# Joined half groups, one ReLU and one subtract moved off VectorE, and a new order at both ends of a top-k attention and highway kernel

## The chip, the cores and the metric

The kernel runs on one core of one Trainium2 chip. The metric is the device time of one execution in microseconds (us), as a median of several runs. Lower is better. TensorE, VectorE (DVE in the profile), ScalarE (ACT), GpSimd (POOL) and SyncE (SP) each take their own instructions in order, and an instruction waits where a semaphore tells it to.

## The reference

The inputs are q, k and v of shape (8 batches, 8 heads, 576 rows, 64), and the weights of one highway layer. Per batch and head the kernel computes the scores, keeps in every row those that reach the row's 32nd largest, and takes the softmax over them:

```python
scores = scale * np.matmul(q, k.transpose(0, 1, 3, 2))
kth = np.partition(scores, -32, axis=-1)[..., -32:-31]
scores = np.where(scores >= kth, scores, -1e9)
attn = softmax(scores) @ v
```

The heads are put side by side, giving x of shape (4608, 512), and the layer follows:

```python
H = np.maximum(x @ w_h, 0.0)
T = 1.0 / (1.0 + np.exp(-(x @ w_t + b_t)))
out = T * H + (1.0 - T) * x
```

## The kernel before, in words

**Tiling.** The 576 query rows of a batch are cut into four groups of 128 rows (`qt` 0 to 3) and a *rest group* of 64 rows (`qt` 4). A full group has 8 tiles, one per head; a rest group has 4 tiles, each holding two heads of 64 rows. Two tiles make a *pair*, two pairs a *quad*. A batch has 18 pairs, so 144 pairs in all, and a written-out loop walks over `step` n = 0 to 149. Pair n passes through stages in successive steps: `scores` and `evac` (step n-1), `tree` (n), `lists` and `lists_rest`, `mask` and `trans` (n+4), `av` (n+5).

**Selecting the 32nd largest.** VectorE does this. `tree` and `folds` take maxima of halves, giving tiles `hi`, `hh`, `h3` (printed as h) and `w2` (printed as w). `minima`, on GpSimd, gets the matching minima with four integer operations per quad at each odd step: hh, hh, hi, hi. `tops` (even steps) and `rest` (odd steps, the last rounds in the next even step as `late`) pull the 8 largest of each list by MAX8 and MATCH_REPLACE8. `settle` keeps, on GpSimd, figures that let the end of the kernel decide whether the lists were long enough; if not, an exact version of the whole kernel runs after it.

**The layer.** When a group's last pair has passed `av`, `norm` divides by the row sums (reciprocal `rinv` on VectorE, the product `x` on GpSimd). Then three pieces are put into the list `ffn`, and each step pops one: `ffn_x` (transposes of x on TensorE; xT and xh on ScalarE), `ffn_h` with `ffn_d` (first product on TensorE, then d = relu(product) - xh by one VectorE instruction), `ffn_t` with `ffn_e` and `ffn_o` (second product, tanh on ScalarE, d = (tanh+1)*d on VectorE, o = x + d on GpSimd, and the store on SP). The TensorE half of a piece (`pre`) stands early in a step, the rest (`post`) late.

**What sets the order.** All compute instructions are pinned to program order on their engine (class `Pinned`). DMAs and the instructions issued before the loop are not. So on GpSimd an instruction written in `post` of an odd step stands behind the four `minima` of that step. I number steps from the first pair of a batch: with n mod 18, full groups reach `norm` at 8, 12, 16 and 20, and the rest group at 22 (which is 4 in the next batch). Its pieces are popped at 24, 25 and 26 (6, 7 and 8 in the next batch), because the group ahead of it uses 21 to 23. So the rest group's `ffn_d` comes at an odd step and its `ffn_e` at the even step right after, while a full group's `ffn_d` comes at an even step.

**Both ends.** At the start, the four head pairs of batch 0 are prepared one after another (`early`): loads of k, q and v (twelve DMAs for each head pair), transposes of k and q through one PSUM buffer (`fps`, one buffer, shared with the layer), copies on ScalarE, and then the scores of the next pair. At the end, after the last pair, the layer of the last full group and of the last rest group runs alone, followed by the checks.

Of the kernel before, what the change touches and what calls it, by code (L numbers as in the profile page):

```python
# [18 lines left out]
WIDE = 600.0  # L19
# [27 lines left out]
class Group:  # L47


    def __init__(self, b, qt, gi, H, P):  # L50
        self.b, self.qt, self.gi = b, qt, gi
        self.rem = qt == J
        self.qlen = P // 2 if self.rem else P
        tiles = (
            [(2 * hp, 2 * hp + 1) for hp in range(H // 2)]
            if self.rem
            else [(h,) for h in range(H)]
        )
        self.nt = len(tiles)
        self.pairs = [tiles[i : i + 2] for i in range(0, self.nt, 2)]  # L60


class Ops:
# [31 lines left out]
    def load_pair(self, src, hp, name, eng=None):  # L95
        nc, D, S, R, P = self.nc, self.D, self.S, self.R, self.P
        JP = J * P
        t = self.ldpool.tile([P, J + 1, 2, D], FP32, tag=name, name=name)
        eng = eng or nc.sync
        for hh in range(2):  # L100
            h = 2 * hp + hh
            eng.dma_start(
                t[:, 0:J, hh, :], src(h, 0, JP).rearrange("(p j) d -> p j d", j=J)
            )
            eng.dma_start(t[0:R, J, hh, :], src(h, JP, S))
        return t
# [6 lines left out]
    def prep_pair(self, srcs, hp, prep, qeng=None):  # L113
# [6 lines left out]
        def load():  # L120
            ins["k"] = self.load_pair(srcs[1], hp, "kin")
            ins["q"] = self.load_pair(srcs[0], hp, "qin", qeng)
            ins["v"] = self.load_pair(srcs[2], hp, "vin")

        def main(name, dst):
            kqps = self.fps.tile([P, 512], FP32, tag="fp", name="kqps")
            for c in range(J):
                nc.tensor.transpose(
                    kqps[:, c * P : (c + 1) * P],
                    ins[name][:, c, :, :].rearrange("p h d -> p (h d)"),  # L130
                    self.ident[:],
                )
            nc.scalar.copy(dst[:, hp, 0:JP], kqps[:])

# [11 lines left out]
        def values():  # L146
            vdst = vb[:, 2 * hp : 2 * hp + 2, :, 0:D].rearrange("p h c d -> p c h d")
            nc.scalar.copy(vdst[:, 0:J], ins["v"][:, 0:J])
            nc.scalar.copy(vdst[0:R, J], ins["v"][0:R, J])
# [51 lines left out]
    def folds(self, k, g, pi):  # L201


        vec, P, S, H = self.nc.vector, self.P, self.S, self.H
        H1, H2, H3 = S // 2, S // 4, S // 8
        if pi == 0:
            g.w2 = self.lpool.tile([P, H, H2 + 24], FP32, tag="w2", name="w2")
        hi, hh, h3 = self.quads[k]
        vec.tensor_tensor(hh[:], hi[:, :, 0:H2], hi[:, :, H2:H1], ALU.max)
        a, b = hh[:, :, 0:H3], hh[:, :, H3:H2]  # L210
        vec.tensor_tensor(h3[:], a, b, ALU.max)
        return vec.tensor_tensor(
            g.w2[:, 2 * pi : 2 * pi + 4, H3:H2], a, b, ALU.min
        )
# [22 lines left out]
    def tops(self, g, t, h3, hl):  # L237
# [5 lines left out]
        m1, m2, w2 = g.m1[:, t, :], g.m2[:, t, :], g.w2[:, t, :]  # L243
# [13 lines left out]
    def rest(self, g, t, lo):  # L257
# [6 lines left out]
        w2 = g.w2[:, t, :]  # L264
# [29 lines left out]
    def lists(self, n, g, pi):  # L294
        P, H = self.P, self.H
        if pi == 0:
            for name in ("m1", "m4") if self.exact else ("m1", "m2", "m4"):
                setattr(g, name, self.lpool.tile([P, H, 8], FP32, tag=name, name=name))
# [19 lines left out]
    def settle(self, g):  # L318
# [7 lines left out]
            self.room[:, g.gi, 0:nt, 0:3],  # L326
            thr.unsqueeze(2).to_broadcast([P, nt, 3]),
# [3 lines left out]
        gp.tensor_tensor(  # L331
            self.slack[:, g.gi, 0:nt, 0], g.m2[:, 0:nt, 7], thr, ALU.subtract
        )
        gp.tensor_copy(self.reach[:, g.gi, 0:nt], g.m1[:, 0:nt, 0])
# [44 lines left out]
    def trans(self, n):  # L379
# [4 lines left out]
        zr = self.zrps.tile([P, 512], FP32, tag="zr", name="zr")  # L384
        for ti in range(2):
            self.chunk_T(zr[:, ti * P : (ti + 1) * P], z, pen, ti, J)
        nc.scalar.activation(
            et[:, :, J, :],
            zr[:, 0 : 2 * P].rearrange("p (t j) -> p t j", t=2),
            AF.Exp,  # L390
            scale=self.scale,
        )
# [10 lines left out]
        self.st[n].update(et=et, zr=zr)  # L403

    def av(self, n, g, pi, vb):
# [4 lines left out]
        if pi == 0:  # L410
            g.xs = self.xpool.tile([P, self.H * DE], FP32, tag="xs", name="xs")
        ql = g.qlen
        c0 = col = 0 if g.rem else 2 * P
        h0 = g.pairs[pi][0][0]
        for ti, heads in enumerate(g.pairs[pi]):
            for hi, h in enumerate(heads):
                q0 = hi * (P // 2)
                for c in range(J + 1):
                    nc.tensor.matmul(
                        zr[0:ql, col : col + DE],  # L420
# [6 lines left out]
        nc.scalar.copy(g.xs[0:ql, h0 * DE : h0 * DE + col - c0], zr[0:ql, c0:col])  # L427
# [3 lines left out]
    def norm(self, g):  # L431
        nc, P, H, D = self.nc, self.P, self.H, self.D
        ql = g.qlen
        xs3 = g.xs[0:ql, :].rearrange("p (h e) -> p h e", e=D + 1)
        rinv = self.xpool.tile([P, H], FP32, tag="rinv", name="rinv")
        nc.vector.reciprocal(rinv[0:ql, :], xs3[:, :, D])
        g.x = self.xpool.tile([P, H * D], FP32, tag="x", name="x")
        nc.gpsimd.tensor_tensor(
# [6 lines left out]
    def ffn_x(self, g):  # L445
        nc, P, n_g, ql = self.nc, self.P, self.n_g, g.qlen
# [16 lines left out]
    def ffn_h(self, g):  # L463
        nc, P, n_g, ql = self.nc, self.P, self.n_g, g.qlen
# [10 lines left out]
    def ffn_d(self, g):  # L475

        ql = g.qlen
        g.d = self.fpool.tile([self.P, self.dm], FP32, tag="d", name="d")
        self.nc.vector.scalar_tensor_tensor(
# [8 lines left out]
    def ffn_t(self, g):  # L488

        nc, P, n_g, ql = self.nc, self.P, self.n_g, g.qlen  # L490
        g.ps = self.fps.tile([P, 512], FP32, tag="fp", name="tps")
# [13 lines left out]
    def ffn_e(self, g):  # L505

        ql = g.qlen
# [9 lines left out]
    def ffn_o(self, g, dst):  # L517
        ql = g.qlen
        o = self.fpool.tile([self.P, self.dm], FP32, tag="o", name="o")
        self.nc.gpsimd.tensor_tensor(o[0:ql, :], g.x[0:ql, :], g.d[0:ql, :], ALU.add)  # L520
        self.nc.sync.dma_start(dst, o[0:ql, :])
# [3 lines left out]
def kernel(  # L525
# [17 lines left out]
    assert D == 64 and R == 64 and H % 4 == 0 and dm == 512  # L543
# [13 lines left out]
    nc.vector.tensor_scalar_mul(nident[:], ident[:], -STEEP)  # L557
# [11 lines left out]
    for i in range(2):  # L569
# [5 lines left out]
    room = const([P, NG, H, 3], FP32, "room")  # L575
    nc.gpsimd.memset(room[:], 1.0)
    slack = const([P, NG, H, 1], FP32, "slack")
    nc.gpsimd.memset(slack[:], 1.0)
    reach = const([P, NG, H], FP32, "reach")
    nc.gpsimd.memset(reach[:], 1.0)  # L580
# [8 lines left out]
        room=room, slack=slack, reach=reach,  # L589
    )  # L590

    with ExitStack() as cm:
# [12 lines left out]
        def srcs(b):  # L605
            return [
                (lambda h, r0, r1, t=t: t[b, h, r0:r1, :]) for t in (q, k, v)
            ]

        def out_rows(g):  # L610
            if not g.rem:
                r0 = g.b * S + g.qt
                return out[r0 : r0 + JP : J, :]
            r0 = g.b * S + JP
            return out[r0 : r0 + R, :]

        groups = [
            Group(b, qt, b * nck + qt, H, P) for b in range(B) for qt in range(nck)
        ]
        pairs = [(g, pi) for g in groups for pi in range(len(g.pairs))]  # L620
# [6 lines left out]
        def prep(b, hp, qeng=None):  # L627
            if hp == 0:
                preps[b] = ops.prep_alloc(vbufs[b % 2])
            return ops.prep_pair(srcs(b), hp, preps[b], qeng)  # L630
# [20 lines left out]
        early = [prep(0, hp, nc.scalar if hp == 0 else None) for hp in range(NHP)]  # L651
# [8 lines left out]
        step = 0  # L660
        late = []
        while step < NPR + 6 or ffn:
            n = step
            if n + 1 < NHP:
                for piece in early[n + 1][1:4]:
                    piece()
                if n + 2 < NHP:
                    early[n + 2][0]()
            if have(n):
                ops.tree(n)  # L670
                if n % 2:
                    ops.minima(n // 2, ops.folds(n // 2, *pairs[n - 1]))
            if n == 1:
# [3 lines left out]
            post = None  # L677
            if ffn:
                pre, post = ffn.pop(0)
                pre()  # L680
# [3 lines left out]
            if have(n - 4):  # L684
# [7 lines left out]
            ended = have(n - 5) and pairs[n - 5][1] == len(pairs[n - 5][0].pairs) - 1  # L692
# [8 lines left out]
            else:  # L701
# [3 lines left out]
                if post:  # L705
                    post()
                if ended:
                    ops.norm(pairs[n - 5][0])
                ops.run(gens)
            if have(n - 4):  # L710
# [7 lines left out]
            if ended:  # L718
# [6 lines left out]
                        lambda g=g: (ops.ffn_e(g), ops.ffn_o(g, out_rows(g))),  # L725
# [3 lines left out]


        ok = const([P, 4], FP32, "ok")
        vec = nc.vector
        vec.tensor_reduce(ok[:, 0:1], room[:], op=ALU.min, axis=AX.XYZ)
        vec.tensor_reduce(ok[:, 1:2], slack[:], op=ALU.min, axis=AX.XYZ)
        vec.tensor_reduce(ok[:, 2:3], reach[:], op=ALU.max, axis=AX.XY)
        bad = const([P, 4], FP32, "bad")
        vec.tensor_scalar(bad[:, 0:1], ok[:, 0:1], TINY, None, ALU.is_lt)
        vec.tensor_scalar(bad[:, 1:2], ok[:, 1:2], 0.0, None, ALU.is_lt)
        vec.tensor_scalar(bad[:, 2:3], ok[:, 2:3], WIDE, None, ALU.is_gt)
        vec.tensor_reduce(bad[:, 3:4], bad[:, 0:3], op=ALU.max, axis=AX.X)  # L740
        bps = ops.fps.tile([P, 512], FP32, tag="fp", name="bps")
        nc.tensor.transpose(bps[0:1, 0:P], bad[:, 3:4], ident[:])
        flag_f = const([1, 1], FP32, "flag_f")
        vec.tensor_reduce(flag_f[:], bps[0:1, 0:P], op=ALU.max, axis=AX.X)
        flag = const([1, 1], I32, "flag")
        vec.tensor_copy(flag[:], flag_f[:])

    taken = nc.values_load(flag[0:1, 0:1], min_val=0, max_val=1)
    with tc.If(taken > 0):
        with tc.For_i(0, B, 1) as b:  # L750
            with ExitStack() as cm:
                ops = Ops(cm, tc, shared, exact=True)
                srcs = [
                    (lambda h, r0, r1, t=t: t[bass.ds(b, 1), h, r0:r1, :].rearrange("o s d -> (o s) d"))
# [58 lines left out]
```

## Time and profile before

| | us |
|---|---|
| median of 3 runs | 925.96 |
| lowest, highest | 923.73, 926.5 |
| the profiled run, timed | 925.72 |
| span of its trace | 923.9 |

The engines' instructions stand mostly under line 35, the line of the helper that pins them, so they are told apart by their tiles. In a row of the groups, the tile left of the arrow is written, those right of it are read; the first number is the total busy time in us, the second the mean of one instruction in ns, and what follows the bar is the engine's idle time ahead of them. TensorE is busy for 79% of the span, ScalarE for 76%, GpSimd for 77%. The granted TensorE clock is 0.944 of full speed in the mean.

From the DVE timeline I take the start of each `hi` instruction (the tree of one step). Between the tree of step 3 (34.54 us) and that of step 143 (881.42 us), VectorE is idle for about 5 us in all. One quad (two steps) takes between 11.30 us and 13.33 us, depending on which parts of the layer fall into it.

### The profile page before, as it was taken

Reading aid. Unit: us, or ns where it says so; the run is one execution under the profiler, and the core shown is the slowest. Engines: PE = TensorE matmul, PEld = TensorE weight load, DVE = VectorE, ACT = ScalarE, POOL = GpSimd, SP = SyncE. Lnnn points to the kernel's source line nnn. Section 1 sums busy time; section 2 is a strip of 40 time slices with the busy share of each in tenths; the row PEclk is TensorE's granted clock in tenths of the full one; section 3 lists DMA queues with packets and bytes.
Section 4 is the critical chain, followed back from the end, with each engine's and each line's share of the span. In section 5 each row is a group of like instructions: output and inputs, shape, how many; then the busy total and the mean of one; then the engine's idle time right before and its main releaser. Section 6 shows DMA issues by size and latency. Waiting matters only on the chain.

```text
span 923.9 us, 20386 instructions
## 1 busy us (share of the span) xinstructions
PE 730.8 (79%) x6601; PEld 510.6 (55%) x6601; DVE 873.4 (95%) x4234; ACT 699.2 (76%) x1321; POOL 709.5 (77%) x509
## 2 busy tenths in 40 slices
PE   5687878878788887878888787887879878877774
PEld 3355556555565555555655555655646555555552
DVE  4699999999999999999999999999999999999991
ACT  3488778887787886887878886888868878776772
POOL 3777778877877888777788887887787778877761
PEclk9999899999999998998999999999989989998997
DMA  5731220221103220122202212023100300000000
GB/s 114 138 70 40 51 51 13 58 69 45 38 18 69 61 52 12 46 51 51 51 13 56 50 41 51 13 67 73 46 24 25 71 12 13 12 13 7 13 24 21
DMA packets 123298, 40.33 MB, mean 44 GB/s; under 512 B 117424, under 2 KB 118576, under 8 KB 123184
## 3 DMA queue, kind: packets, MB, share of 16 engines
q1 hardware_dynamic: 120768, 37.48, 16.6%
q0 software_dynamic: 1200, 1.18, 0.8%
q8 instruction: 54, 0.88, 0.4%
q14 instruction: 60, 0.49, 0.2%
q10 hardware_dynamic: 1216, 0.30, 0.1%
HBM read 30.67 MB, written 9.44 MB: 43 GB/s over the span
## 4 chain that ended last, share of the span: by engine, by line
DVE 78%; POOL 8%; PE 7%; ACT 3%; issue 2%; SPq 1%; DMA 1%; POOLq 0%; ACTq 0%; DVEq 0%
DVE w L35 37%; DVE m L35 18%; DVE hi L35 9%; DVE hh L35 6%; DVE d L35 5%; POOL hi L35 4%; DVE h L35 3%; PE ps L35 2%; POOL hh L35 2%; PE zt L35 2%; POOL o L35 1%; PE zr L35 1%; PE xtps L35 1%; POOL x L35 1%; PE kqps L35 1%
## 5 line engine op out<-in xcount | busy, mean ns | idle before, releaser
L35 PE MATMUL ps<-kT,qT 64*128 64x64 f32 (+3 forms) x1280 | 221.9, 473 | 48.8 <-DVE hi L35 47.8
L35 ACT ACTIVATE z<-ps 128x1152 f32<-128x1152 f32 x144 | 163.0, 1132 | 96.7 <-PE ps L35 95.6
L35 POOL TENSOR_TENSOR hh<-hi,hh 128x576 int32<-128x576 int32 x72 | 101.6, 1410 | 171.9 <-DVE w L35 171.7
L35 PE MATMUL zt<-ident,z 128*128 128x128 f32 x1152 | 225.1, 289 | 0.0
L35 ACT ACTIVATE pen<-z,m 128x576 bf16<-128x576 f32 x288 | 224.1, 779 | 0.2 <-DVE m L35 0.2
L35 PE MATMUL zt<-nident,pen 128*128 128x128 bf16 x1152 | 214.5, 226 | 0.0
L35 DVE MAX8 m<-w 128x8 f32<-128x168 f32 (+1 forms) x864 | 203.6, 283 | 0.0
L35 PEld LDWEIGHTS ps<-kT,qT 64*128 64x128 f32 (+1 forms) x1280 | 112.8, 191 | 148.2 <-issue 88.5
L35 POOL TENSOR_TENSOR hi<-hi,z 128x1152 int32<-128x1152 int32 x72 | 190.1, 2641 | 5.6
L35 POOL TENSOR_TENSOR hi<-z,hi 128x1152 int32<-128x1152 int32 x72 | 189.3, 2629 | 5.6
L35 PEld LDWEIGHTS zt<-ident,z 128*128 128x128 f32 x1152 | 169.8, 147 | 18.4
L35 ACT ACTIVATE et<-zt 128x512 bf16<-128x512 f32 x288 | 161.9, 602 | 15.5 <-PE zt L35 14.1
L35 PEld LDWEIGHTS <-pen 128*128 128x128 bf16 x1440 | 161.0, 112 | 6.3 <-ACT pen L35 6.3
L35 DVE MATCH_REPLACE8 w<-m,w 128x72 f32<-128x72 f32 (+1 forms) x576 | 148.3, 265 | 0.0
L35 DVE TENSOR_TENSOR hi<-ps,z 128x576 f32<-128x576 f32 x144 | 106.3, 738 | 21.6 <-ACT z L35 21.5
L35 DVE MAX8 w<-hi 128x8 f32<-128x288 f32 x288 | 116.5, 445 | 0.0
L35 POOL TENSOR_TENSOR hh<-hh,hi 128x576 int32<-128x576 int32 x72 | 101.4, 1408 | 5.6
L35 PEld LDWEIGHTS <-et 128*128 128x128 bf16 (+1 forms) x1600 | 70.4, 104 | 36.3 <-ACT et L35 13.8
L35 PE MATMUL zr<-v,et 128*128 128x65 bf16 (+1 forms) x1600 | 82.4, 199 | 5.1 <-ACT et L35 4.9
L35 DVE MAX8 w<-hh 128x8 f32<-128x72 f32 x576 | 83.9, 216 | 0.0
L35 PE MATMUL zr<-ident,z 128*128 128x128 f32 x288 | 76.8, 320 | 3.9 <-ACT xs L35 3.9
L35 PE MATMUL xtps<-ident,x 128*128 128x128 f32 (+1 forms) x160 | 28.0, 304 | 60.4 <-POOL x L35 51.1
(64 smaller groups left out, 1102.7 us busy)
## 6 DMA issues: line engine op xcount, KB each, us to landing
kin<-in_k_dram SPq DMA_DIRECT2D x64, 128.0 KB, 2.7
vin<-in_v_dram SPq DMA_DIRECT2D x64, 128.0 KB, 2.6
out_dram<-o SPq DMA_DIRECT2D x32, 256.0 KB, 2.3
qin<-in_q_dram SPq DMA_DIRECT2D x62, 128.0 KB, 2.6
kin<-in_k_dram SPq DMA_DIRECT2D x64, 16.0 KB, 2.5
vin<-in_v_dram SPq DMA_DIRECT2D x64, 16.0 KB, 2.3
out_dram<-o SPq DMA_DIRECT2D x8, 128.0 KB, 2.3
qin<-in_q_dram SPq DMA_DIRECT2D x62, 16.0 KB, 2.4
```

The source lines that it names most:

```text
L35: return self._tc.keep_in_program_order(fn(*args, **kw))
```

## The change

1. **Joint rests.** The rest groups of two neighbouring batches share one tile of 128 rows. The even batch's group writes rows 0 to 63 and gets no layer pieces; after the odd batch's group wrote rows 64 to 127, one `norm`, one layer and two stores serve both.
2. **ReLU and subtract.** For all groups but the last, `ffn_d` becomes a ScalarE Relu from PSUM into d and a GpSimd subtract of xh in place.
3. **One-op checks.** `settle` has one GpSimd instruction where it had three; the second list of maxima m2 lies behind w2 for this. The final checks are rewritten and issued at step 148, their last part ahead of the last `ffn_e`.
4. **Start.** The k and q transposes of batch 0 use the `zt` PSUM buffers; the q copy is on VectorE; ScalarE's queue carries the second head of the first k and of the first q; rests of both heads are one DMA, and both heads of v are one; `nident` is written by ScalarE; the weights load at step 5; the tree of a step stands ahead of the early pieces.
5. **End.** From step 147 on, both masks come first, the main transposes precede the ends, and the layer's TensorE part comes behind `av` and `trans`. The last group uses VectorE for d, x and o, and a `zt` buffer for its second product.

The core of the diff:

```diff
     def ffn_d(self, g):
 
-        ql = g.qlen
+        ql = g.rows
         g.d = self.fpool.tile([self.P, self.dm], FP32, tag="d", name="d")
+        if not self.exact and not g.final:
+            self.nc.scalar.activation(g.d[0:ql, :], g.ps[0:ql, :], AF.Relu)
+            self.nc.gpsimd.tensor_tensor(
+                g.d[0:ql, :], g.d[0:ql, :], g.xh[0:ql, :], ALU.subtract
+            )
+            return
         self.nc.vector.scalar_tensor_tensor(
...
-            ended = have(n - 5) and pairs[n - 5][1] == len(pairs[n - 5][0].pairs) - 1
+            ended = False
+            if have(n - 5):
+                g, pi = pairs[n - 5]
+                ended = pi == len(g.pairs) - 1 and (not g.rem or g.r0 > 0)
...
-            nc.scalar.copy(dst[:, hp, 0:JP], kqps[:])
+            if early and name == "q":
+                nc.vector.tensor_copy(dst[:, hp, 0:JP], kqps[:])
+            else:
+                nc.scalar.copy(dst[:, hp, 0:JP], kqps[:])
...
-                ins["k"] = self.load_pair(srcs[1], hp, "kin")
-                ins["q"] = self.load_pair(srcs[0], hp, "qin", qeng)
+            if qeng:
+                ins["k"], k_rest = self.load_pair(srcs[1], hp, "kin", None, qeng)
+                ins["q"], q_rest = self.load_pair(srcs[0], hp, "qin", None, qeng)
+                k_rest()
+                q_rest()
...
         gp.tensor_tensor(
-            self.room[:, g.gi, 0:nt, 0:3],
-            thr.unsqueeze(2).to_broadcast([P, nt, 3]),
+            self.room[:, g.gi, 0:nt, :],
+            thr.unsqueeze(2).to_broadcast([P, nt, 4]),
             ends,
             ALU.subtract,
         )
-        gp.tensor_tensor(
-            self.slack[:, g.gi, 0:nt, 0], g.m2[:, 0:nt, 7], thr, ALU.subtract
-        )
-        gp.tensor_copy(self.reach[:, g.gi, 0:nt], g.m1[:, 0:nt, 0])
...
-    nc.vector.tensor_scalar_mul(nident[:], ident[:], -STEEP)
+    nc.scalar.mul(nident[:], ident[:], -STEEP)
...
+            if final and have(n - 4):
+                ops.mask(n - 4, *pairs[n - 4], tis=(1,))
             if ffn:
                 pre, post = ffn.pop(0)
-                pre()
+                if not final:
+                    pre()
...
+            if final:
+                if have(n - 4):
+                    ops.trans(n - 4, final=True)
+                if pre:
+                    pre()
...
+                if n == NPR + 4:
+                    judge_lists()
                 if ended:
                     ops.norm(pairs[n - 5][0])
+                if n == NPR + 4:
+                    judge_scales()
```

## The prediction

> **What bounds the kernel now.** I read the page first: the busy times, then the chain of waits.
>
> ```profile
> PE 730.8 (79%) x6601; PEld 510.6 (55%) x6601; DVE 873.4 (95%) x4234; ACT 699.2 (76%) x1321; POOL 709.5 (77%) x509
> ...
> DVE 78%; POOL 8%; PE 7%; ACT 3%; issue 2%; SPq 1%; DMA 1%; POOLq 0%; ACTq 0%; DVEq 0%
> ```
>
> DVE leads in both. The shares hide three stages, so I cut the span where the tree of step 3 starts (34.54 us) and where that of step 143 does, using the busy times by stretch (PE, PEld, DVE, ACT, POOL after the length; then clock, DMA share, GB/s).
>
> ```profile
> 0.00:34.54 34.54, 19.14 (x72) 12.12 (x72) 14.64 (x39) 13.72 (x28) 18.12 (x25) 1.00 0.53 114
> 34.54:129.66 95.12, 76.82 (x673) 54.08 (x673) 93.47 (x465) 74.34 (x143) 72.23 (x49) 0.95 0.33 71
> 129.66:881.42 751.76, 610.42 (x5636) 428.38 (x5636) 743.08 (x3640) 590.63 (x1113) 603.20 (x419) 0.95 0.15 38
> 881.42:923.90 42.48, 24.44 (x220) 16.01 (x220) 22.25 (x94) 20.48 (x40) 15.98 (x17) 0.82 0.07 24
> ```
>
> From 34.54 to 881.42 DVE is 99% busy: there a DVE instruction taken away shortens the time, if nothing makes DVE wait instead. In the head (34.54 us) and the tail (42.48 us) nobody is full, so the order of dependent steps counts.
>
> **What the skill says.** "GPSIMD Engine Reference", section Engine selection: two-input work is about twice as slow as on VectorE. The trace agrees: o costs 1269 ns on POOL, the DVE instruction d 681 ns.
>
> ```profile
> L35 POOL TENSOR_TENSOR o<-x,d 128x512 f32<-128x512 f32 x32 | 40.6, 1269 | 3.9 <-DVE d L35 3.9
> L35 DVE SCALAR_TENSOR_TENSOR d<-hps,xh 128x512 f32<-128x512 f32 x32 | 21.8, 681 | 6.2 <-PE hps L35 6.2
> L35 ACT ACTIVATE xh<-x 128x512 f32<-128x512 f32 x32 | 19.9, 622 | 0.0
> ```
>
> "SBUF — State Buffer", section Who interferes with whom: a DVE instruction with two SBUF inputs contends with a GpSimd instruction that reads SBUF. The fold hh is one. Where POOL's x runs into it, it takes 0.92 us instead of the 0.76 seen elsewhere, so the trace agrees, at 0.15 us for 0.3 us of overlap:
>
> ```profile
> 93.10 0.92 DVE L35 TENSOR_TENSOR hh<-hi 128x576 f32<-128x576 f32 x1
> ```
> ```profile
> 92.36 1.04 POOL L35 TENSOR_TENSOR x<-xs,rinv 128x512 f32<-128x512 f32 x1
> ```
>
> **Middle stage, term by term.** Tree starts in the DVE timeline give quad lengths. A quad without layer work takes 11.30 us; with one d 11.87; with e and rinv 11.96. So d or e is worth 0.57 us of DVE's time (instructions overlap a little) and rinv 0.09.
>
> *d of the full groups and first rests.* The first batch has 3 d's in this stage: -1.7. Each later batch has d in the quads of steps 3, 9, 13 and 17 and, for the rest, 7: -0.57 each.
>
> *Rests.* After batches 0, 2, 4 and 6 no rest layer runs: quad 3 loses rinv too, quad 7 falls from 12.55 to 11.36 (d and e gone; a rinv of the next group stays). Such a batch period loses 0.66+1.19+3x0.58 = 3.6 us. There are four, the last without its quad 17 (behind step 143): -13.8.
>
> *The joint rest after batches 1, 3 and 5.* Here the subtract adds a wait. A rest's d comes at an odd step (25), behind the four minima in POOL's order, and its e at the next even step. Today in such a quad, tree at 165.57:
>
> ```profile
> 173.73 2.64 POOL L35 TENSOR_TENSOR hi<-hi,z 128x1152 int32<-128x1152 int32 x1
> 176.33 1.27 POOL L35 TENSOR_TENSOR o<-x,d 64x512 f32<-64x512 f32 x1
> ```
> ```profile
> 170.16 0.66 DVE L35 SCALAR_TENSOR_TENSOR d<-hps,xh 64x512 f32<-64x512 f32 x1
> ...
> 175.02 0.67 DVE L35 SCALAR_TENSOR_TENSOR d<-tps,d 64x512 f32<-64x512 f32 x1
> ```
>
> d runs on DVE at +4.59 from the tree, in the middle of the minima. The subtract can only start where they end, at 176.33 (+10.76), and takes 1.27 (o's time): ready at 177.6. DVE reaches e at 175.02 - 0.57 = 174.45. It stalls 3.15 us; behind e stand rinv, the tops and the next tree. Bounds: 0, if e turned out later; 3.5 with slower POOL. I take 3.15. Besides, at step 22 POOL now has the subtract of group 3 ahead of the rest's x, which moves x into the next fold by about 0.9 us: +0.7 (0 to 0.9). Such a period: quads 3, 9, 13, 17 -0.57 each, quad 7 -0.57+3.15, quad 5 +0.7, together +1.0. Three: +3.0.
>
> *Do full groups stall?* Their d is at an even step: the subtract runs at +10.9 to +12.2 of the quad, while e comes 4.6 us into the next one, at +15.9. The margin is 3.7 us, so no. POOL's room (one instruction instead of three, at most 0.3 us) ends at +12.4, and the next fold starts at about +12.1 to +12.2: 0.05 us (0 to 0.5) in 23 quads, +1.2.
>
> *ScalarE.* Relu costs about 0.62 (xh's row); "ScalarE: Activation LUTs", section What ACT_TABLE_LOAD costs, prices 512 elements with immediates at 186 + 0.833x512 = 613 ns, an estimate. Behind it stand the exps and the next step's masks. ACT has idle time ahead of the following z in most steps, and z leads the tree by 1 to 3 us; hidden, except where a low TensorE clock has used that lead already (z at 0.04 us in three quads 13): d's gain shrinks by 0.35 there, +1.0.
>
> Middle: -1.7 - 13.8 + 3.0 + 1.2 + 1.0 = **-10.3 us**.
>
> One-op checks free POOL (slack and reach, 20 us busy), and TensorE and ScalarE lose four layer passes: costed at nothing, as DVE sets the pace. Weights at step 5 cost POOL 2.3 us, which fit into its gap before the minima at +2.5 of the next quad.
>
> **Head.**
>
> ```profile
> 5.63 1.09 PE L35 MATMUL kqps<-ident,kin 128*128 128x128 f32 x4 [5.63 <-DMA kin<-in_k_dram]
> 7.39 1.12 PE L35 MATMUL kqps<-ident,qin 128*128 128x128 f32 x4 [0.68 <-ACT kT L35]
> 9.18 0.37 PE L35 MATMUL kqps<-ident,kin 64*128 64x64 f32 x1 [0.68 <-ACT qT L35]
> ```
> ```profile
> 13.01 0.76 DVE L35 TENSOR_TENSOR hi<-ps,z 128x576 f32<-128x576 f32 x1 [4.43 <-ACT z L35]
> ...
> 19.83 0.76 DVE L35 TENSOR_TENSOR hi<-ps,z 128x576 f32<-128x576 f32 x1 [6.06 <-ACT z L35]
> ```
>
> A single PSUM buffer makes the q transposes wait for the copy of k, and those of the next pair for z, the v cast (0.81) and kT. The third DMA of k is issued at 2.40 and lands at 5.6. On ACT's queue the second k goes at about 0.76 and lands 3.2 us later, at 4.0. Then: k and q transposes 2.2, q copy on DVE 0.67 (like hi, less 64 elements), copy to end of scores 2.66 (9.13 to 11.79 today), z and hi 1.25: first hi at 10.85 instead of 13.01. A round becomes 1.12+1.12+0.05+0.67+2.66 = 5.6 us instead of 6.8 (the last one 7.9, waiting for DMA). Step 3's tree: 10.85+3x5.6 = 27.7, which is also when the tops queued ahead of it end (q copy 23.75+3.85). Gain 6.8. Loads: eight issues of 0.62 per pair on SP fit into a round, where twelve took 7.8. Moving nident frees DVE at a time when it is idle; on ACT I take it to stand behind the two DMAs, as POOL's trace shows a ready memset issued ahead of an unready select. Were it ahead, 2 us are lost. **-6.8** (-3 to -8).
>
> **Tail.** ACT and TensorE run one step after the other; Relu adds 0.5 at step 144. At step 147 both masks together and main chunks first take some 1.4 off; last `av` ends 0.9 earlier than 906.63. From there: product 1.05, Relu 0.6, second product 1.3, tanh 0.6, e 0.7 of group 3, then (one `fps` buffer) xtps 0.5, xT 0.6, product 1.05, second product 1.3 (its own buffer), tanh 0.6, e and o on DVE 0.7 each: 9.8, where the trace has 906.63 to 917.24 = 10.6. The second store adds one issue, 0.5. DVE's checks lie in its idle time. **-1.2** (-4 to +1).
>
> Sum: -6.8 - 10.3 - 1.2 = -18.3 against the span 923.9, i.e. 905.6. The timed runs lie near that (median 925.96; the profiled run took 925.72 for a 923.9 span), so the same difference gives **907.7 us**.
>
> **Rivals.**
> - *No stall at the joint rest* (the subtract gets done in time, or slower folds put e behind it). For: margins of 3.7 us elsewhere; against: POOL's order. Saves 3x3.15 and 3x0.7: 896.
> - *The head is bound by transfers.* For: 114 GB/s and a DMA share of 0.53 today, with waits on kin and qin in the last round; against: fewer issues. Head -2.5: 912.
> - *POOL and DVE collide at every fold*, subtract or room holding hh 0.5 us longer in 23 quads: +11.5, 919.
> - *Slower than before: the subtract gates e in full groups too.* One mechanism: POOL, held up by folds or by Relu, finishes the subtract late. Room took 0.73 instead of 0.25 us in the folds, so delays exist. Stalls start from a delay of 3.7 us; 4.6 us would cost 0.9 in 31 groups, +28, net +9.6: 935.6.
>
> **How the numbers follow.** Main case 0.56 (own range 903 to 912), no stall 0.14, head 0.14, collisions 0.12, slower 0.04. The range 895.5 to 915.5 leaves out the last two. About 0.3% is what a measurement of this kernel can tell from no change. Faster 0.95, within 0.01, slower 0.04.
>
> **What would show it.** d<-hps on DVE once, not 40 times; d<-tps 36; Relu and POOL d 35 each. DVE waiting on POOL d three times for some 3 us, and nowhere else. Tree of step 3 near 27.7. hh below 0.85 us in the mean. I am wrong if quads 9 stay at 11.9 us, if DVE waits for POOL in full groups, or if the early rounds stay near 6.8.

## The result and the profile after

| | before | after |
|---|---|---|
| median, us | 925.85 (4 runs) | 911.41 (4 runs) |
| lowest to highest, us | 923.73 to 926.5 | 909.43 to 914.86 |
| ratio of the times, 95% interval | | 0.9852 [0.9817, 0.9887] |
| span of the profiled run, us | 923.9 | 913.1 |

The change saves 14.4 us in the median. The profiled run of the kernel after was its slowest (914.86 us), so the traces show only 10.8 of these. All positions below are from the profiled runs.

The busy times and the chain of waits, from the page of the kernel after:

```profile
PE 728.1 (80%) x6549; PEld 508.0 (56%) x6549; DVE 856.8 (94%) x4192; ACT 709.5 (78%) x1341; POOL 732.8 (80%) x454
...
DVE 67%; POOL 16%; PE 10%; ACT 4%; issue 1%; DMA 1%; SPq 1%; POOLq 0%; ACTq 0%; DVEq 0%
```

DVE lost 16.6 us of work, but its share of the chain fell from 78% to 67% and GpSimd's doubled from 8% to 16%. So part of the work that left DVE came back as waiting for GpSimd. The busy times by stretch, cut at the trees of steps 3 and 143 as in the prediction (length, then PE, PEld, DVE, ACT, POOL, clock, DMA share, GB/s):

```profile
0.00:26.40 26.40, 15.99 (x72) 10.31 (x72) 10.20 (x42) 12.19 (x26) 14.72 (x22) 1.00 0.66 157
26.40:871.44 845.04, 686.96 (x6250) 481.41 (x6251) 823.75 (x4058) 674.40 (x1271) 702.42 (x421) 0.94 0.16 41
871.44:913.10 41.66, 25.20 (x230) 16.30 (x228) 22.81 (x94) 22.89 (x45) 15.62 (x13) 0.82 0.09 28
```

The head fell from 34.54 to 26.40 us (-8.1) and the tail from 42.48 to 41.66 (-0.8). The middle went from 846.88 (95.12 + 751.76) to 845.04: only -1.8, although DVE has 12.8 us less to do there (836.55 to 823.75). The other 11.0 us are idle time of DVE: length less busy time rose from 10.3 to 21.3 us (this counts the short gaps between instructions too; the waits above 0.15 us alone, the "about 5 us" of the kernel before, rose from 5.3 to 16.5). And the 12.8 us are themselves too few: at the prediction's prices, the 37 d's, four e's and four rinv's that left this stage are worth 23.7 us. What took back the rest is in the groups, and in the waits. First the fold hh in the kernel before, then the kernel after:

```profile
L35 DVE TENSOR_TENSOR hh<-hi 128x576 f32<-128x576 f32 x72 | 58.2, 808 | 2.5
```
```profile
L35 DVE TENSOR_TENSOR hh<-hi 128x576 f32<-128x576 f32 x72 | 68.9, 958 | 2.5
...
L35 POOL TENSOR_TENSOR d<-d,xh 128x512 f32<-128x512 f32 x35 | 44.5, 1271 | 23.9 <-ACT d L35 23.8
```
```profile
POOL d L35 <- ACT d L35: 23.8, 12, 6.2
...
DVE d L35 <- POOL d L35: 9.4, 3, 3.1
```

Three things are to be seen. First, DVE waits for the subtract at e three times, 9.4 us in all: the joint rests. Second, the fold hh takes 68.9 us instead of 58.2 in the same 72 instructions (958 ns in the mean, 808 before). This is lost time inside an instruction, so it counts as busy and no view of waits shows it. Without these 10.7 us DVE's busy time in the middle would have fallen by 23.5, as priced. Third, GpSimd waits for Relu twelve times (23.8 us). That wait costs GpSimd nothing by itself, but it decides when the subtract runs.

**Where it happens.** From the DVE timeline I took the starts of all trees and summed the quads by the place of their first step in a batch (n mod 18). The predicted column sorts the terms of the prediction by place:

| quad | before, us | after | difference | predicted |
|---|---|---|---|---|
| 1, 11 and 15 | 274.99 | 281.96 | +7.0 | +1.2 |
| 3 | 98.43 | 94.89 | -3.5 | -4.4 |
| 5 | 94.38 | 97.81 | +3.4 | +2.1 |
| 7 | 99.52 | 102.36 | +2.8 | +3.0 |
| 9 | 95.02 | 90.30 | -4.7 | -4.6 |
| 13 | 100.32 | 97.65 | -2.7 | -3.6 |
| 17 | 84.22 | 80.07 | -4.2 | -4.0 |
| sum | 846.88 | 845.04 | -1.8 | -10.3 |

Quads 7, 9 and 17 came out as predicted. Quad 3 fell less than predicted, but e5 below, the same program run again, has 91.7 us there, so that part differs from run to run. Quad 15 alone grew by 6.2 us: it took 12.8 instead of 12.0 us in seven of eight batches, with hh at 1.62 us instead of 0.76. What comes before such a quad, in its quad 13 (steps 31 and 32, trees at 190.96 and 197.36), engine by engine, from the timeline of the kernel after:

```profile
192.10 1.12 PE L35 MATMUL xtps<-ident,x 128*128 128x128 f32 x4 [2.51 <-POOL x L35]
...
193.69 2.40 PE L35 MATMUL ps<-kT,qT 64*128 64x512 f32 x8
...
201.39 1.30 PE L35 MATMUL ps<-kT,qT 64*128 64x512 f32 x8
```
```profile
202.79 1.13 ACT L35 ACTIVATE z<-ps 128x1152 f32<-128x1152 f32 x1 [0.36 <-PE ps L35]
203.82 0.59 ACT L35 ACTIVATE d<-hps 128x512 f32<-128x512 f32 x1
```
```profile
199.28 2.64 POOL L35 TENSOR_TENSOR hi<-hi,z 128x1152 int32<-128x1152 int32 x1
204.49 1.27 POOL L35 TENSOR_TENSOR d<-d,xh 128x512 f32<-128x512 f32 x1 [2.57 <-ACT d L35]
```
```profile
203.95 0.76 DVE L35 TENSOR_TENSOR hi<-ps,z 128x576 f32<-128x576 f32 x1 [0.98 <-ACT z L35]
204.74 1.62 DVE L35 TENSOR_TENSOR hh<-hi 128x576 f32<-128x576 f32 x1
```

TensorE waits 2.51 us for x, which stands on GpSimd behind the minima and o. Its next instructions run long (xtps 1.12, the scores 2.40 us), and as it takes them in order, the scores of the step after start late too, at 201.39. Relu stands behind z on ScalarE, and this z waits for those scores. So Relu ends at 204.4. The minima had been done at 201.92, but the subtract only starts at 204.49, and hh, which starts 0.25 us later, is held up by 0.86 us. My theory: besides the stall at the joint rests, **the late Relu shifts the subtract into the next fold**, and the late x stands at the head of that chain. The rivals: the joint rest's stall is the one loss that counts, and GpSimd slows the folds whatever the order; or what is missing is lost to TensorE's low clock, wherever Relu stands. Each expectation below was written before its run.

### The profile page after: what moved, and what is told of

Read it like the earlier page. It is cut to its first block, busy times and chain, and to the rows that moved or that the text cites. A ratio compares the mean times of both kernels' runs of the same rounds, so it can differ in the third digit from the quotient of the medians.

```text
span 913.1 us, 19940 instructions
## 1 busy us (share of the span) xinstructions
PE 728.1 (80%) x6549; PEld 508.0 (56%) x6549; DVE 856.8 (94%) x4192; ACT 709.5 (78%) x1341; POOL 732.8 (80%) x454
## 4 chain that ended last, share of the span: by engine, by line
DVE 67%; POOL 16%; PE 10%; ACT 4%; issue 1%; DMA 1%; SPq 1%; POOLq 0%; ACTq 0%; DVEq 0%
DVE w L35 35%; DVE m L35 12%; DVE hi L35 8%; POOL hi L35 8%; DVE hh L35 6%; POOL hh L35 4%; PE ps L35 4%; DVE h L35 3%; PE zr L35 2%; DVE d L35 2%; ACT z L35 1%; POOL o L35 1%; PE xtps L35 1%; PE zt L35 1%; POOL x L35 1%
## 5 line engine op out<-in xcount | busy, mean ns | idle before, releaser
L35 PE MATMUL ps<-kT,qT 64*128 64x64 f32 (+3 forms) x1280 | 227.1, 482 | 50.7 <-DVE hi L35 47.1
L35 ACT ACTIVATE z<-ps 128x1152 f32<-128x1152 f32 x144 | 163.0, 1132 | 94.9 <-PE ps L35 93.3
L35 PE MATMUL zt<-ident,z 128*128 128x128 f32 x1152 | 220.8, 285 | 0.0
L35 PE MATMUL zt<-nident,pen 128*128 128x128 bf16 x1152 | 210.4, 223 | 0.0
L35 PEld LDWEIGHTS zt<-ident,z 128*128 128x128 f32 x1152 | 167.2, 145 | 16.9
L35 DVE MAX8 m<-w 128x8 f32<-128x168 f32 x576 | 160.9, 322 | 0.0
L35 PEld LDWEIGHTS <-et 128*128 128x128 bf16 (+1 forms) x1600 | 74.1, 105 | 36.5 <-ACT et L35 18.3
L35 PE MATMUL zr<-v,et 128*128 128x65 bf16 (+1 forms) x1600 | 86.6, 200 | 8.0 <-ACT et L35 5.6
L35 DVE MATCH_REPLACE8 w<-m,w 128x168 f32<-128x168 f32 x288 | 89.6, 320 | 0.0
L35 PE MATMUL xtps<-ident,x 128*128 128x128 f32 x144 | 28.9, 334 | 59.7 <-POOL x L35 55.9
```

Of the source, the lines that this page charges most:

```text
L35: return self._tc.keep_in_program_order(fn(*args, **kw))
```

## The experiments

**Without one cost each.** e1 puts d of the joint rests back on DVE:

```diff
-        if not self.exact and not g.final:
+        if not self.exact and not g.final and not g.joint:
             self.nc.scalar.activation(g.d[0:ql, :], g.ps[0:ql, :], AF.Relu)
```

> The d of the joint rest groups goes back to one VectorE instruction; all else is as after the change (911.4 us). Theory A (VectorE stands still at three joint rests because the subtract waits behind the four minima): three waits of 3.13 us go, three d's of 0.57 us come back, so -7.7 us, about 904, and no wait of DVE for POOL d is left. Theory B (the time of a quad is set by TensorE and ScalarE, VectorE's waits only show it): the time comes back as waits for z, at most -2 us, 909 or more.

Measured: 901.67 us (900.19 to 902.6), 0.9751 of before [0.973, 0.9773]. The row of e, in the groups of e1:

```profile
L35 DVE SCALAR_TENSOR_TENSOR d<-tps,d 128x512 f32<-128x512 f32 x36 | 24.2, 673 | 1.3 <-ACT tps L35 1.3
```

The wait for POOL's d is gone, and quad 7 of a joint rest takes 12.55 us instead of 15.17: 2.6 us three times, 7.9 us in all, as theory A has it. The time fell by 9.7 us against 911.4, 2 more than expected: in the trace the quads 13 fell too, from 97.65 to 93.2 us. None of them takes 13 us any more, as three did; why, no run shows. Quad 15 still takes 12.84 us in five of eight batches, so the loss in the fold does not come from the stall. The quads 13 at steps 85 and 121 are a test of their own: TensorE waits 2.5 us for x there as well, but the scores take 1.30 us, the subtract starts 10.97 and 10.95 us after the tree, and the next hh takes 0.87 and 0.86 us. So it is the slow TensorE behind the wait, more than the wait itself, that makes Relu too late.

e2 splits Relu off and issues it ahead of the scores and of z; the subtract stays where it was:

```diff
+                    (
+                        lambda g=g: ops.ffn_h(g),
+                        lambda g=g: g.final or ops.ffn_r(g),
+                        lambda g=g: ops.ffn_d(g),
+                    ),
...
+            if mid:
+                mid()
             if have(n + 1):
```

> The Relu stands ahead of the copy of the scores (z) on ScalarE, not behind it; the subtract keeps its place. Theory A (where TensorE's clock is low the Relu behind z comes 1.4 to 2.6 us late, the subtract then runs into the next fold hh and holds it 0.86 us): in quads 13 the subtract starts at about +11 and not at +12.3 to +13.5, hh in the quads 15 falls from 1.62 to below 1.0 us, -5 to -7 us, about 905. Theory B (the folds are slow for another reason, or z is delayed as much as the Relu gains): within 2 us of 911.4.

Measured: 902.11 us (898.68 to 904.48), 0.9753 [0.9725, 0.9782]. The row of hh in the groups of e2:

```profile
L35 DVE TENSOR_TENSOR hh<-hi 128x576 f32<-128x576 f32 x72 | 60.1, 835 | 2.4
```

GpSimd now waits for Relu 8.6 us in all instead of 23.8. In seven of eight quads 13 the subtract starts where the minima end, and the next hh takes 0.76 to 0.84 us. Quad 15 falls to 12.0 to 12.2 us everywhere. The TensorE gap ahead of xtps is still there, and quad 13 still takes about 11.8 us in five of eight batches: the clock has a share of its own, but the loss in the fold goes with the place of Relu. The gain of 9.3 us against 911.4 is above the 5 to 7 expected; between the traces, quads 15 give 4.6 us of it and quads 13 another 2.7.

e3 takes the ReLU and the subtract of all groups back to DVE's single instruction, and keeps all else of the change:

```diff
-        if not self.exact and not g.final:
+        if False:
```

> Every d is again one VectorE instruction; joint rests, checks and both ends stay as after the change. Theory A (the moved d saves 0.57 us in 34 quads, 19.4 us, but waits of 9.4 us at the joint rests and about 10 us of collisions with folds eat it): within 3 us of 911.4. Theory B (the move is worth its whole VectorE time and the missing gain lies elsewhere): 19 us slower, about 930.

Measured: 913.04 us (911.53 to 913.67), 0.9877 [0.9854, 0.9899]. The changed kernel itself, run again as e5 below, has 0.9873 [0.9852, 0.9894]. The intervals overlap almost wholly: **in the change as made, moving ReLU and subtract off DVE was worth nothing that these runs can tell.** The sum of hh is 58.4 us, quad 9 is back at 11.87 and quad 15 at 11.96. By stage it is not nothing: the middle of e3 takes 840.4 us, less than the changed kernel's (845.0, and 843.6 in e5), and its tail 44.1 us, more than the changed kernel's (41.7 and 39.1). So in the middle the move cost 3 to 5 us, and the tail gave them back.

e4 goes to the start of the chain. o of a group is issued behind the x that follows it on GpSimd, so that TensorE gets x earlier:

```diff
+                for g in outs:
+                    ops.ffn_o(g, *out_rows(g))
+                outs.clear()
...
-                            ops.ffn_o(g, *out_rows(g)),
+                            ops.ffn_o(g, *out_rows(g)) if g.final else outs.append(g),
```

> o of a full group is issued one step later, behind x of the next group, so that x starts 1.27 us earlier and TensorE waits less for it. Theory A (the idle gap of 2.5 us ahead of the transposes of x is what brings the low TensorE clock in quads 13, and with it the late Relu and the late z): gap about 1.3 us, no slow transposes in quads 13, subtract at about +11 there, -5 to -9 us, 902 to 906. Theory B (the low clock comes from something else): the same number of slow stretches and within 2 us of 911.4.

Measured: 897.96 us (896.95 to 898.77), 0.9715 [0.9693, 0.9736]. The same step as above in the timeline of e4 (its tree at 189.16):

```profile
189.06 0.66 PE L35 MATMUL xtps<-ident,x 128*128 128x128 f32 x4 [1.28 <-ACT v L35]
...
189.97 1.30 PE L35 MATMUL ps<-kT,qT 64*128 64x512 f32 x8
...
195.90 1.30 PE L35 MATMUL ps<-kT,qT 64*128 64x512 f32 x8
```
```profile
198.33 0.59 ACT L35 ACTIVATE d<-hps 128x512 f32<-128x512 f32 x1
```
```profile
200.08 1.28 POOL L35 TENSOR_TENSOR d<-d,xh 128x512 f32<-128x512 f32 x1
```
```profile
201.39 0.81 DVE L35 TENSOR_TENSOR hh<-hi 128x576 f32<-128x576 f32 x1
```

With x early, TensorE waits 1.28 us instead of 2.51; xtps takes 0.66 and the scores 1.30 us, and the next scores start 6.7 us after the tree instead of 10.4; Relu ends before the minima do, the subtract starts 10.92 us after the tree, as the prediction had it, and hh takes 0.81. Quads 13 sum to 91.6 us (97.65 after), quads 15 to 96.1 (101.9), quads 3 to 92.2 (94.9; but 91.7 in e5, so this part is not the edit's). The gain of 13.4 us against 911.4 is above the 5 to 9 expected: 6.0 and 5.8 of it are in the quads 13 and 15. In the middle DVE waits for z no more. The three stalls of the joint rests stay (9.4 us). In the quads 13 the chain is cut at its first link. It is not gone everywhere: at steps 83 and 119 (quads 11) a late subtract still holds hh at 1.12 and 1.24 us.

**The change again, and all three edits.** e5 is the changed kernel once more, beside the same runs of before as the next ones. e6 is e1, e2 and e4 together.

> The changed kernel once more, unaltered, beside the kernel before on this chip: ratio 0.9852 within its interval (0.982 to 0.989). In its trace three waits for POOL d of 3.1 us, and slow transposes of x in most of the quads 13, if the low clock there belongs to the kernel; in other quads, or in fewer, if it depends on how the clock's changes fall in a run.

Measured: 912.09 us (910.04 to 914.9), 0.9873 [0.9852, 0.9894]. Quad 15 takes 12.84 us in seven of eight batches again, and the joint rests stall DVE for 9.35 us, so neither is an accident of one execution. Of the expected slow transposes there are fewer: xtps is slow (1.11 to 1.12 us) in four quads 13, where after it was seven, but the scores behind it are long (2.38 to 2.40 us) in all seven that have the gap. At steps 29, 65 and 101 (quads 11) hh takes 1.23 to 1.25 us beside a late subtract, which the first trace does not have. So how the low clock falls does change from run to run, and the loss in quads 15 stays.

> d of the joint rests on VectorE, Relu ahead of z, and o behind x, all three. If the waits at the joint rests are independent of the collisions in quads 15, and the last two repairs remove the same collisions: gain over the changed kernel 8 us plus 11.6 us, some 19 us, a ratio to the kernel before of about 0.964. If all three remove the same waits, no better than o behind x alone (0.9715).

Measured: **889.49 us** (888.42 to 891.38), 0.9628 [0.9611, 0.9645], 22.6 us below e5 and so below both kernels. The middle of e6, as a stretch:

```profile
26.51:848.82 822.31, 666.89 (x6258) 470.50 (x6259) 817.49 (x4062) 672.49 (x1273) 693.80 (x419) 0.96 0.17 43
```

The middle is at 822.3 us, 22.7 less than after, and DVE is busy for 99% of it (817.49). Its busy sum fell from 823.75 to 817.49 although the kernel has three DVE instructions more (4195 against 4192): most of that is hh, 63.0 us in e6 against 68.9. The middle is 8.0 us shorter than that of e4, and 7.8 of these are in the quads 7 of the joint rests. So once o stands behind x, Relu ahead of z adds nothing that the trace shows, as the expectation allowed: the two remove the same collisions.

e9 is e6 with all ReLUs and subtracts on DVE, the counterpart of e3:

```diff
-        if not self.exact and not g.final and not g.joint:
+        if False:
```

> As with the three repairs, but every d is one VectorE instruction again, so that the only difference is where the d of the 32 full groups but those at the end is computed. If the move is worth VectorE's time once nothing waits for it: 30 d's of 0.57 us, 17 us slower than the three repairs (889.5 us), about 906.5, less up to 1.5 us of fold collisions with the subtracts. If the move's worth was lost to something other than the waits: within 5 us of 889.5.

Measured: 905.74 us (905.38 to 906.69), 0.9796 [0.9782, 0.9809]: 16.2 us slower than e6. That is near the 17 us expected (30 d's in the middle at 0.57 us), but the traces, which are 17.8 us apart, divide it otherwise. The quads 3, 9, 13 and 17, which hold the 30 d's, are 17.6 us longer in e9, so each d costs what the prediction took. The other quads are 4.2 us shorter, because the subtracts and the x behind them no longer hold the fold (hh 58.4 us in all, 63.0 in e6). That leaves 13.3 us in the middle. The tail adds 4.4 us: d stands on DVE ahead of the last group's rinv and x and waits for its product, so that the transposes of that x come 2.3 us later, and after that TensorE runs at a low clock in e9 (hps 1.89 us, 1.04 in e6). So **each moved d was worth what DVE's time says, once nothing waits for it; in the change as made, waits and held folds took more than that in the middle.** That the whole comes so near to 17 us is in part luck.

**The other parts.** e7 undoes the joint rests: each batch has its own rest layer again, with its subtract on GpSimd.

```diff
-            ends = [(g.b + i) * S for i in (0, 1)]
+            ends = [(g.b + 1) * S]
...
-            Group(b, qt, b * nck + qt, H, P, joint=True)
+            Group(b, qt, b * nck + qt, H, P)
...
-                ended = pi == len(g.pairs) - 1 and (not g.rem or g.r0 > 0)
+                ended = pi == len(g.pairs) - 1 and (not g.rem or not g.joint or g.r0 > 0)
```

> The rest groups are not joined: each gets its own layer, with Relu and subtract; all else is as after the change. Theory A (at every rest the subtract waits behind the minima): seven waits of 3.1 us and not three, so +12.5, four e's and rinv's more, +2.6, four more collisions of x with a fold, +3: some 18 us slower than the changed kernel. Theory B (only the instructions of four layer passes count): 2.6 us slower on VectorE, at most 5.

Measured: a median of 937.07 us, 1.0143 [1.0125, 1.0162], slower than before. Of its five runs four lie between 937.0 and 938.17 and one at 927.39; the profile is of that one. Its DVE waits:

```profile
DVE d L35 <- POOL d L35: 21.9, 7, 3.1
```

Seven rests stall 3.13 us each, instead of three, and all seven quads 7 that hold one take 15.2 us. The profiled span is 16.4 us above e5's, near the 18 us of theory A; the median is 25.0 us above. So the joining saves not only layer work but also four stalls, and the rest of the change without it is slower than before. The further 10 us of the other four runs are in no trace, and their cause stays open.

e8 keeps the new loads but takes the start's transposes back to the single `fps` buffer and the q copy back to ScalarE:

```diff
-            prep(0, hp, nc.scalar if hp == 0 else None, True) for hp in range(NHP)
+            prep(0, hp, nc.scalar if hp == 0 else None) for hp in range(NHP)
```

> In the first four head pairs k and q go through the single fps buffer again and ScalarE copies q; loads, nident and the order of the steps stay as after the change. If the buffers and the copy make the head's gain: rounds of 6 to 7 us, tree of step 3 near 31 us and not 26.4, 4 to 5 us slower. If the fewer and earlier loads make it: tree of step 3 within 1 us of 26.4.

Measured: 918.13 us (915.4 to 920.38), 0.9928 [0.991, 0.9946], 6.0 us slower than e5. First the starts of the trees in the DVE timeline of e8, then in that of the kernel after:

```profile
11.61 0.76 DVE L35 TENSOR_TENSOR hi<-ps,z 128x576 f32<-128x576 f32 x1 [11.61 <-ACT z L35]
18.42 0.76 DVE L35 TENSOR_TENSOR hi<-ps,z 128x576 f32<-128x576 f32 x1 [6.05 <-ACT z L35]
...
32.05 0.76 DVE L35 TENSOR_TENSOR hi<-ps,z 128x576 f32<-128x576 f32 x1 [2.28 <-ACT z L35]
```
```profile
11.34 0.76 DVE L35 TENSOR_TENSOR hi<-ps,z 128x576 f32<-128x576 f32 x1 [3.74 <-ACT z L35]
...
16.51 0.76 DVE L35 TENSOR_TENSOR hi<-ps,z 128x576 f32<-128x576 f32 x1 [3.74 <-ACT z L35]
...
20.63 0.76 DVE L35 TENSOR_TENSOR hi<-ps,z 128x576 f32<-128x576 f32 x1 [1.12 <-ACT z L35]
...
26.40 0.75 DVE L35 TENSOR_TENSOR hi<-ps,z 128x576 f32<-128x576 f32 x1
```

With one buffer a round takes 6.81 us, as it did before (13.01 to 19.83); with the pair of buffers and the copy on DVE 4.1 to 5.8. The first tree is early in both (11.61; 13.01 before), so that part doesn't need the buffers. The last round of e8 takes 6.81 too, where before it took 7.90 waiting for DMA. So of the head's 8.1 us, buffers and q copy together make 5.7 (32.05 against 26.40), and the loads and the new order 2.5; what the buffers are worth without the copy was not tried. Nor does any run take back the one-op checks or the new order at the end alone, so their shares are not shown.

## Why the prediction was right, point by point

The time was 911.4, the prediction 907.7, inside its range. Its sum was -18.3; the trace gave -10.8, the medians -14.4. That the range held owes something to its width of 20 us: the largest term, -10.3 for the middle, came to -1.8 (-3.3 in e5). Of the signs it named, the counts of d, the three waits of 3.1 us, quads 9 and the early rounds came true; the mean of hh, which was to stay below 0.85 us, was 0.958.

- **Head, -6.8: right in mechanism, too small (-8.1, just past its own bound of -8).** k landed at 4.29 us (4.0 predicted), the q copy took 0.69 (0.67), the first tree came at 11.34 (10.85), the rounds took 5.17, 4.12 and 5.77 (5.6). The second round was the mis-sized one: I had priced all rounds with TensorE as slow as at the start, and there the scores took 1.30 us instead of 2.40. nident stood behind the two DMAs on ScalarE, as taken, and took 0.31 us. e8 confirms what makes the rounds. The rival of transfers that bind the head fell: TensorE waits 1.34 us for qin in the last round, but step 3's tree follows on DVE without a gap.
- **d of the groups, -0.57 each: right.** Quads 9 and 17 went to 11.28 and 11.43 us. e9 against e6 has 17.6 us for 30 in the quads that hold them.
- **The stall at the joint rest, 3.15 us: right (3.13, three times).** The trace of one, at the end of the minima, POOL first:

```profile
272.58 2.64 POOL L35 TENSOR_TENSOR hi<-hi,z 128x1152 int32<-128x1152 int32 x1
275.17 1.26 POOL L35 TENSOR_TENSOR d<-d,xh 128x512 f32<-128x512 f32 x1
```
```profile
276.47 0.69 DVE L35 SCALAR_TENSOR_TENSOR d<-tps,d 128x512 f32<-128x512 f32 x1 [3.13 <-POOL d L35]
```

  The x pushed into the fold of quad 5 cost 0.76 (0.7 predicted) in these three; a fourth quad 5, at step 131, was held by a late subtract.
- **Fold contention, "+1.2": the step that failed.** I let the subtract run where the minima end (+10.9 from the tree), and took 0.05 us per quad. In seven of eight quads 13 it ran at +12.3 or +13.5, because it waited for Relu, and in the quad 15 behind each of these, and once in a quad 5 (step 131), the fold lost 0.86 us: 8 x 0.86 = 6.9 us. With the 2.3 us of the joint rests and 0.6 of one fold at step 3, 0.9 of the 10.7 us is left for the small contention that the term was meant for. "ScalarE. Relu ... hidden" was true of the time that Relu takes on ScalarE (0.59 us, where its two prices were 0.62 and 0.61), and false of its place: I asked what Relu delays, not what delays Relu. The same sentence had priced the late z of quads 13, and let the Relu that stands right behind this z be on time. The rival of collisions at every fold named the mechanism and misplaced it: they come behind a late z, eight times rather than 23, and cost 0.86 us rather than 0.5.
- **Low TensorE clock at quads 13, "+1.0": too small, measured +1.9** (-2.7, where d alone gives -4.6). Three of them lose 1.5 us against e4's 11.45, four 0.35.
- **Tail, -1.2: -0.8.** The two products of the last group took 1.9 us each, where I had 1.05 and 1.3 from the tail before. That is the clock's doing, and the near hit is luck: e5, the same program, has the same tail up to the transposes of the last x (26.54 us into it in both traces), and then products of 1.04 and 1.03 us and a tail of 39.1 us, -3.4. Its tail as a stretch, to be held against the 41.66 us at 0.82 above:

```profile
870.14:909.22 39.08, 22.73 (x230) 15.59 (x228) 22.88 (x94) 22.72 (x44) 15.63 (x13) 0.93 0.10 30
```

- **Slower than before: no.** DVE never waited for the subtract of a full group; in the middle delays of 2.6 us did not use up the margin of 3.7.

The Trainium skill, "SBUF — State Buffer", section Who interferes with whom, calls the port pair that DVE and GpSimd share an exclusive lock. The trace agrees: beside the hh that took 1.62 us, the subtract took its usual 1.27. The rule gives no time that DVE is held; the traces do: hh loses the overlap less some 0.15 us (0.16 for 0.30 us of overlap with x in the prediction's example, 0.76 for 0.91 beside the x in quads 5, 0.86 for 1.02 beside the subtract). And whichever starts second is held: room, which starts 0.97 us into the long hh, takes 0.78 us, where it takes 0.28 outside a fold.

## What to carry to other kernels

When work moves from the engine that sets the pace to two others in series, look up for both where the new instruction stands in its queue and what the one ahead of it waits for; its duration alone says nothing. A wait that costs its own engine nothing still decides which instructions collide, and a collision shows as a longer instruction, not as idle time, so compare the mean of untouched instructions before and after. If a move of 17 us brings nothing, cut the waits one by one before dropping it: here o behind x (or Relu ahead of z) and three d's back on VectorE gave most of it back.

## What the runs showed of the hardware

- The Trainium skill, "TensorE: Matmul & The Clock Gate", section Part 1: The HAM clock gate, gives some 3.4 us as the window over which TensorE's activity is judged. Here gaps of 2.5 us were enough. The kernel after has one ahead of xtps in seven of eight quads 13, and behind each of them xtps took 1.02 to 1.12 us instead of 0.66 and the scores ran long (2.40 instead of 1.30 in the step shown). In the kernel before it was five of seven such gaps, in e1 five of seven too. Behind the gaps of 1.2 to 1.3 us at this place in e4 none ran long. Taking 1.2 us from the gap thus took another 1.6 us from the instructions behind it in the step shown (0.46 from xtps, 1.10 from the scores). But 2.5 us is no threshold: in the kernel after TensorE waits only 1.33 us up to 50.33, and from 51.43 us its clock is at 0.50 for 3.41 us. The record of the clock agrees with the window's length: the middle of that trace has 26 stretches at 0.50, each 3.41, 6.83 or 10.24 us long.
- One kernel (e7) has two levels of time, 927.4 and 937 to 938, in five runs of the same program. Their granted clocks in the mean are 0.929 and 0.923 to 0.924; whether that makes the difference stays open.
